# Expert 0's last row blocks between its second-layer products, and expert 1's weight splits spread over two experts

## The chip, the cores and the metric

The kernel runs on one core of a Trainium2 chip. The metric is the device time of one execution in microseconds (us); the lower, the better. The engines are named as the profile names them: PE (TensorE), DVE (VectorE), ACT (ScalarE), POOL (GpSimd) and SP (SyncE, which issues most transfers).

## What is computed

A recurrent attention over 4 batches, 8 heads and 768 steps gives an array of 3,072 rows by 320 columns, and a layer of 8 experts follows it. Each row goes to the one expert with the highest gate score, and the result is scaled by that score's probability:

```python
logits = x @ w_gate
expert_idx = np.argmax(logits, axis=1)
...
for e in range(E):
    mask = expert_idx == e
    xe = x[mask]
    h = np.maximum(xe @ w1[e], 0.0)      # 320 -> 1024
    ye = h @ w2[e]                       # 1024 -> 320
    out[mask] = gate_w[mask, None] * ye
```

## The kernel before

The attention takes the first 378 us of the profiled execution and is not touched. Near its end it has prepared the first 256 rows of expert 0 and split that expert's first-layer weights. The change lies in `moe`, in the first two of its eight experts.

**One expert.** Each expert has up to 448 rows (four row blocks, q = 0 to 3: three of 128 and one of 64); the five experts with most rows take this many and the others 384. Rows and weights are float32, and PE multiplies them in a faster format that drops low bits, so each operand is split into a rounded high part and the remainder, and three products replace one.

- `split(e)` returns seven pieces: three `s1(k)` for the first-layer weights and four `s2(k)` for the second. Each piece is one copy on ACT (L892 or L896, the high part) and one subtraction on DVE (L893 or L897, the low part). The raw weights come into `w1r` and `w2r` (`load_w1`, `load_w2`: L828, L833, L836). There is one buffer of each, so the transfer for the next expert waits until the last piece of this one has read it.
- `xprep(e, q)` turns one row block: three transposes on PE (L909) into one of two PSUM buffers `xt`, then in a chain ACT (L910, high part of the first 256 columns), DVE (L911, low part), ACT (L913, last 64 columns), DVE (L914).
- `l1(e, g, r)`, g = 0 to 3, is a quarter of the first layer, two blocks of 128 hidden units over the rows r: 16 products on PE (L927 to L931), then for each block a relu on ACT (L933) and the low part on DVE (L937).
- `l2(e, q)` is the second layer of one row block: 24 products (L949 to L951), and 16 for the block of 64 rows (L954 to L957). DVE scales the result (L964; L960 for the block of 64, after ACT's L959), and POOL writes the rows out by an indirect transfer (L965).
- `check(i)` reads an eighth of the raw decay array through the one buffer `WR` (L975, 480 KB) and takes its minimum and maximum on DVE (L976, L977). `within` is six short DVE operations (L877 to L882). Both feed a flag that is read only at the end.

**What sets the order.** In `moe`, the order of PE, ACT and DVE is the order of the program (`manual_schedule`), and each runs its list in that order. SP and POOL are not in that list: a planner places their instructions. The exception is the first `load_w1(1)`.

**The opening.** Expert 0's first 256 rows go through `l1(0, g, slice(0, 256))`, and behind each quarter one piece of that expert's second-layer weights is split. Then come `l2(0, 0)` and `l2(0, 1)`, the range check 0, `xprep` of row blocks 2 and 3, the first layer over rows 256 to 447, and then for each q one `xprep(1, q)`, two pieces of expert 1's split, and (q = 2, 3) the second layer of expert 0. From expert 1 on, the first layer covers all rows at once; two pieces of the next expert's split stand behind each quarter, and one `xprep` of the next expert stands before each `l2`.

Of the kernel before, what the change touches and what calls it, by code (L numbers as in the profile page):

```python
# [24 lines left out]
E = 8  # L25
# [760 lines left out]
def moe(tc, nc, d, ctx, X, out, okt, okv, oki, slots, first, cnts, consts, weights):  # L786
# [27 lines left out]
    def ps(tag, bufs):  # L814
        return PS.tile([128, 512], F32, name="m_" + tag, tag=tag, bufs=bufs)
# [3 lines left out]
    rows = lambda e: CAP if e < NBIG else SMALL  # L819

    def fetch(e):
        at[e] = nc.values_load(perm[0:1, e:e + 1], engines={mybir.EngineType.SP}, min_val=0, max_val=E - 1,
                               skip_runtime_bounds_check_because="perm is a permutation of the experts")

    def load_w1(e):
        w1 = d["w1"][which(e)]
        for k in range(2):
            x = DMA.dma_start(w1r[k], w1[:, k * 128:k * 128 + 128].rearrange("o p f->p (o f)"))  # L828
            if e == 1 and k == 0:
                tc.add_manual_dep(x.ins, gathered[-1].ins.name, mybir.DependencyInfo(  # L830
                    mybir.DependencyClass.Sync, mybir.DependencyReason.DATA))
        for h in (0, 64):
            DMA.dma_start(w1r[2][h:h + 64], w1[:, 256:320].rearrange("o p f->p (o f)"))  # L833

    def load_w2(e):
        DMA.dma_start(w2r, d["w2"][which(e)].rearrange("o (k p) m->p (o k) m", p=128))  # L836

    def load_w(e):
        load_w1(e)
        load_w2(e)  # L840

    def load_x(e):
        for q in range(0 if e else 2, (rows(e) + 127) // 128):
            ix = first[:, q - 2:q - 1] if e == 0 else idx[:, e, q:q + 1]
            x = G_.indirect_dma_start(out=XG[e % 2][:, q, :], out_offset=None, in_=X[0:NT + 1],
                                      in_offset=IndirectOffsetOnAxis(ap=ix.bitcast(U32), axis=0),
                                      bounds_check=NT, oob_is_err=False)
            if e == 0:
                gathered.append(x)
# [37 lines left out]
    def split(e):  # L887
        w1h, w1l = W1[e % 2]
        w2h, w2l = W2[e % 2]

        def s1(k):
            A.copy(w1h[k], w1r[k])  # L892
            V.tensor_tensor(w1l[k], w1r[k], f(w1h[k]), ALU.subtract)  # L893

        def s2(k):
            A.copy(w2h[:, k:k + 2], w2r[:, k:k + 2])  # L896
            V.tensor_tensor(w2l[:, k:k + 2], w2r[:, k:k + 2], f(w2h[:, k:k + 2]), ALU.subtract)  # L897

        return [lambda k=k: s1(k) for k in range(3)] + [lambda k=k: s2(k) for k in range(0, 8, 2)]

    def xprep(e, q):
        xg = XG[e % 2]
        xh, xl, x2 = XH[e % 2]
        n = 128 if q < 3 else 64
        cs = slice(q * 128, q * 128 + n)
        t = ps("xt", 2)[:, 0:384].rearrange("p (k i)->p k i", k=3)
        for k in range(3):
            kw = 128 if k < 2 else 64
            TE.transpose(t[:kw, k, 0:n], xg[0:n, q, k * 128:k * 128 + kw], ident[0:n, 0:n])  # L909
        A.copy(xh[:, :, cs], t[:, 0:2, 0:n])  # L910
        V.tensor_tensor(xl[:, :, cs], t[:, 0:2, 0:n], f(xh[:, :, cs]), ALU.subtract)  # L911
        yield
        A.copy(x2[0:64, 0, cs], t[0:64, 2, 0:n])  # L913
        V.tensor_tensor(x2[64:128, 0, cs], t[0:64, 2, 0:n], f(x2[0:64, 0, cs]), ALU.subtract)  # L914
        if q * 128 + n == rows(e):
            V.tensor_copy(tok[e % 2][:, 0 if e else 2:q + 1], xg[:, 0 if e else 2:q + 1, DM])
# [23 lines left out]
    def l2(e, q):  # L940
        w2h, w2l = W2[e % 2]
        n = 128 if q < 3 else 64
        qs = slice(q * 128, q * 128 + n)
        yp = ps("yp", 2)[:, 0:DM]
        sc = (xg0 if e == 0 and q < 2 else XG[e % 2])[:, q, DM + 1:DM + 2]
        yo = YO[q % 2]
        for ft in range(8):
            if n == 128:
                TE.matmul(yp, hh[:, ft, qs], w2h[:, ft], start=ft == 0, stop=False)  # L949
                TE.matmul(yp, hh[:, ft, qs], w2l[:, ft], start=False, stop=False)  # L950
                TE.matmul(yp, hl[:, ft, qs], w2h[:, ft], start=False, stop=ft == 7)  # L951
            else:
                if ft:
                    TE.matmul(yp[0:n], hh[:, ft, qs], w2l[:, ft], start=False, stop=False)  # L954
                TE.matmul(yp, hx[:, ft, 384:512], w2h[:, ft], start=ft == 0, stop=ft == 7)
                if not ft:
                    TE.matmul(yp[0:n], hh[:, ft, qs], w2l[:, ft], start=False, stop=False)  # L957
        if n < 128:
            A.activation(yt, yp[64:128], AF.Copy, scale=sc[64:128])  # L959
            V.scalar_tensor_tensor(yo[0:n], yp[0:n], sc[0:n], yt, ALU.mult, ALU.add)  # L960
        elif e == E - 1 and q == 2:
            A.activation(yo, yp, AF.Copy, scale=sc)
        else:
            V.tensor_scalar(yo, yp, sc, None, ALU.mult)  # L964
        x = G_.indirect_dma_start(  # L965
            out=out, out_offset=IndirectOffsetOnAxis(ap=tok[e % 2][0:n, q:q + 1].bitcast(U32), axis=0),
            in_=yo[0:n], in_offset=None, bounds_check=NT - 1, oob_is_err=False)
        for y in written:
            tc.declare_no_dep(x.ins, y.ins, reason="they write different rows")
        written.append(x)  # L970
# [3 lines left out]
    def check(i):  # L974
        DMA.dma_start(WR, d["w_raw"][:, i * n:(i + 1) * n])  # L975
        V.tensor_reduce(st[:, i:i + 1], WR, AX.X, ALU.min)  # L976
        V.tensor_reduce(st[:, E + i:E + 1 + i], WR, AX.X, ALU.max)  # L977

    def verdict(last):
        if not last:  # L980
            V.tensor_scalar(st[:, 0:E], st[:, 0:E], WLO, None, ALU.is_ge)
            V.tensor_scalar(st[:, E:2 * E], st[:, E:2 * E], WHI, None, ALU.is_le)
            V.tensor_reduce(okt[:, 1:2], st, AX.X, ALU.min)
            return
        p = ps("xt", 2)[0:1, 0:3]
        TE.matmul(p, okv[:, 0:1], okt, start=True, stop=True)
        V.tensor_reduce(okv[0:1, 1:2], p, AX.X, ALU.min)
        V.tensor_scalar(oki, okv[0:1, 1:2], 127.5, None, ALU.is_ge)

    with tc.manual_schedule(engines={mybir.EngineType.PE, mybir.EngineType.Activation, mybir.EngineType.DVE}):  # L990
        load_w2(0)
        DMA.dma_start(ident, d["cident"])
        load_x(0)
        order()
        for g in range(4):
            l1(0, g, slice(0, 256))
            split(0)[3 + g]()
        V.tensor_copy(tok[0][:, 0:2], xg0[:, :, DM])
        parts = [xprep(0, q) for q in (2, 3)]
        for q in range(2):  # L1000
            l2(0, q)
        check(0)
        for x in parts:
            next(x)
        for x in parts:
            next(x, None)
        for e in range(E):
            todo = split(e + 1) if 0 < e < E - 1 else []
            for g in range(4):
                l1(e, g, slice(0 if e else 256, rows(e)))  # L1010
                if e == E - 1 and g == 0:
                    check(e)
                for _ in range(2):
                    if todo:
                        todo.pop(0)()
            if e == 0:
                load_w2(1)
                todo = split(1) + [within]
            elif e + 2 < E:
                fetch(e + 2)  # L1020
                load_w(e + 2)
            for q in range((rows(e) + 127) // 128):
                if e + 1 < E and q * 128 < rows(e + 1):
                    list(xprep(e + 1, q))
                    if e == 0:
                        for _ in range(2):
                            if todo:
                                todo.pop(0)()
                elif e == E - 1 and q:
                    verdict(q == 2)  # L1030
                if e or q > 1:
                    l2(e, q)
                if q == 0 and 0 < e < E - 1:
                    check(e)
            if e == 0:
                fetch(2)
                load_w(2)
            if e + 2 < E:
                load_x(e + 2)

# [131 lines left out]
```

## Time and profile before

| | |
|---|---|
| device time, median of 3 runs | 609.2 us (607.48 to 609.25) |
| device time of the profiled execution | 605.91 us |
| its span (first to last instruction) | 604.1 us |
| PE busy in the span | 526.7 us, 87% |
| DVE, ACT, POOL busy | 423.0, 383.1, 262.3 us |
| granted PE clock, mean over the span | 0.947 |

The span is what the trace covers; 1.81 us of the profiled execution's time lie around it. In a line of a timeline, the time in square brackets is how long the engine stood idle before that line, and behind the arrow stands what it waited for. Products on PE overlap, so the distance from one start to the next, and not the duration shown, is what one costs when they follow closely.

### The profile page before, as it was taken

How to read it: one execution, taken by the hardware profiler on the slowest of the kernel's cores; microseconds unless marked ns; L12 is line 12 of the kernel's file. 1: busy time of each engine (PE TensorE's matmuls, PEld its weight loads, DVE VectorE, ACT ScalarE, POOL GpSimd, SP SyncE). 2: the span in 40 equal slices, each digit the busy share in tenths (PEclk: the TensorE clock that was granted, in tenths of full speed). 3: DMA queues.
4: the chain of work that ended last, by engine and by line, in shares of the span. 5: the costliest groups of instructions: out<-in, count | busy, mean ns of one | idle time of the engine just before them, and what ended most of it. 6: DMA issues, size and time to landing. Idle time of an engine off the chain costs nothing.

```text
span 604.1 us, 22198 instructions
## 1 busy us (share of the span) xinstructions
PE 526.7 (87%) x9302; PEld 476.2 (79%) x9311; DVE 423.0 (70%) x732; ACT 383.1 (63%) x931; POOL 262.3 (43%) x417
## 2 busy tenths in 40 slices
PE   1787888885998989799899988987999999999995
PEld 0546777775887888689788887986999999999994
DVE  8998986786698788757356465647848576676741
ACT  4666878897788889958778774325634435263420
POOL 5233578448949847964623023611141322314101
PEclk9997879998799999969879999889999999999998
DMA  7622454363445545443735345644756473645100
GB/s 212 204 78 82 145 151 151 116 190 93 154 126 158 164 125 152 137 134 92 187 90 155 86 130 193 182 164 118 248 166 205 128 223 115 194 127 185 55 9 33
DMA packets 37422, 85.50 MB, mean 142 GB/s; under 512 B 6173, under 2 KB 18206, under 8 KB 37316
## 3 DMA queue, kind: packets, MB, share of 16 engines
q1 hardware_dynamic: 34340, 74.93, 41.5%
q0 software_dynamic: 2704, 8.75, 4.5%
q8 instruction: 76, 1.25, 0.8%
q10 hardware_dynamic: 272, 0.33, 0.1%
q14 instruction: 30, 0.25, 0.1%
HBM read 76.07 MB, written 8.32 MB: 140 GB/s over the span
## 4 chain that ended last, share of the span: by engine, by line
PE 58%; DVE 17%; POOL 8%; issue 7%; DMA 5%; ACT 4%; SPq 1%; POOLq 0%; DVEq 0%; ACTq 0%
PE m_hp L928 4%; PE m_hp L929 4%; PE m_hp L927 4%; PE m_yp L949 4%; PE m_yp L951 4%; PE m_yp L950 4%; PE psY L518 4%; PE ps_g L495 3%; PE psS L427 3%; DVE G L296 2%; POOL tmp L364 2%; DVE FF L294 2%; PE psS L455 2%; PE m_hp L930 2%; PE m_hp L931 2%
## 5 line engine op out<-in xcount | busy, mean ns | idle before, releaser
L965 POOL DMA_INDIRECT out<-yo,tok x29 | 28.7, 991 | 152.9 <-DVE yo L964 106.9
L933 ACT ACTIVATE hx<-m_hp 128x448 fp32r<-128x448 f32 (+3 forms) x72 | 34.8, 485 | 48.5 <-PE m_hp L931 48.5
L949 PE MATMUL m_yp<-w2h,hx 128*128 128x320 f32 x192 | 60.8, 317 | 0.0
L951 PE MATMUL m_yp<-w2h,hx 128*128 128x320 f32 x192 | 59.1, 308 | 0.0
L950 PE MATMUL m_yp<-w2l,hx 128*128 128x320 f32 x192 | 59.1, 308 | 0.0
L937 DVE SCALAR_TENSOR_TENSOR hx<-m_hp,hx 128x384 fp32r<-128x384 f32 (+2 forms) x112 | 40.5, 402 | 22.8 <-ACT hx L933 22.3
L498 DVE TENSOR_TENSOR Y<-ps_g,mask 64x512 f32<-64x512 f32 x48 | 32.9, 685 | 21.7 <-PE ps_g L495 21.1
L325 ACT COPY M2c<-ps_g 32x256 f32<-32x256 f32 x96 | 34.9, 364 | 20.6 <-PE ps_g L317 19.0
L460 DVE TENSOR_TENSOR SVR<-psS,F 40x640 f32<-40x640 f32 x46 | 37.8, 822 | 11.5 <-PE psS L455 8.4
L418 ACT COPY KS<-ps_g 64x320 f32<-64x320 f32 x96 | 40.4, 421 | 8.3 <-PE ps_g L414 6.1
L303 POOL TENSOR_TENSOR lend<-lend,FF 128x1024 f32<-128x1024 f32 x12 | 28.5, 2372 | 38.4 <-DVE FF L294 32.9
L364 POOL TENSOR_TENSOR tmp<-Tt 128x28 f32<-128x28 f32 (+6 forms) x70 | 40.8, 583 | 4.9
L446 ACT COPY SVS<-psU 32x320 f32<-32x320 f32 x96 | 40.0, 417 | 4.5 <-PE psU L442 2.7
L471 ACT COPY KS<-ps_g 40x320 f32<-40x320 f32 x92 | 38.5, 419 | 2.8 <-PE ps_g L467 1.3
L518 PE MATMUL psY<-Y,KS 128*40 128x32 f32 x1504 | 34.2, 203 | 5.3 <-DVE Y L498 2.3
L296 DVE TENSOR_TENSOR_SCAN G<-Wt,RC 128x528 f32<-128x528 f32 x21 | 38.1, 1816 | 0.7
L518 PEld LDWEIGHTS psY<-Y,KS 128*40 128x40 f32 x1504 | 31.3, 122 | 8.4 <-issue 4.5
L455 PE MATMUL psS<-SVS,KS 128*40 128x40 f32 x1472 | 33.9, 208 | 3.0 <-ACT SVS L446 1.6
L950 PEld LDWEIGHTS m_yp<-w2l,hx 128*128 128x128 f32 x192 | 36.1, 188 | 0.0
L949 PEld LDWEIGHTS m_yp<-w2h,hx 128*128 128x128 f32 x192 | 36.0, 188 | 0.0
L951 PEld LDWEIGHTS m_yp<-w2h,hx 128*128 128x128 f32 x192 | 36.0, 187 | 0.0
L495 PE MATMUL ps_g<-RT,VU 128*64 128x64 f32 x768 | 31.2, 237 | 4.7 <-DMA Wt<-in_W 2.4
(248 smaller groups left out, 1532.9 us busy)
## 6 DMA issues: line engine op xcount, KB each, us to landing
w2r<-in_w SPq DMA_DIRECT2D x8, 1280.0 KB
lend<-in_w SPq DMA_DIRECT2D x16, 512.0 KB
VU<-in_VT SPq DMA_DIRECT2D x48, 160.0 KB
SVR<-in_VR SPq DMA_DIRECT2D x48, 104.0 KB
SVS<-in_VS SPq DMA_DIRECT2D x24, 208.0 KB
lend<-in_w SPq DMA_DIRECT2D x16, 256.0 KB
RT<-in_RT SPq DMA_DIRECT2D x48, 80.0 KB
Y<-in_RY SPq DMA_DIRECT2D x24, 160.0 KB
```

The source lines that it names most:

```text
L296: V.tensor_tensor_scan(back(at(G, s)), back(w), back(RC), 0.0, ALU.mult, ALU.max)
L364: V.tensor_tensor(t, bcast(0, j, 32, 0), bcast(j, j + 1, 0, 1), ALU.mult)
L418: A.copy(halves(ks[0:64, u * 8 + z:u * 8 + 8:2]), halves(ts[u][64 * z:64 * z + 64]))
L446: A.copy(halves(sv[32:64, 4 * v:4 * v + 4]), by_type(solved[32 * v:32 * v + 32]))
L455: TE.matmul(psS[TR[ty], h, j * 40:j * 40 + 40], ks[:, p, o:o + 40], sv[:, p, o:o + 40], start=True, stop=True, tile_position=(0, o))
L471: A.copy(ks[64:104, 8 * z:8 * z + 8, TO[ty]:TO[ty] + 40], ts[ty][64 * z:64 * z + 40])
L495: TE.matmul(a[z:z + 64, :, x], vu[:, p, :], rt[:, :, p, :], start=True, stop=True, tile_position=(0, z))
L518: TE.matmul(py[TR[ty], p], ks[:, p, o:o + 40], y2[:, ty, p, :], start=True, stop=True, tile_position=(0, o))
L937: V.scalar_tensor_tensor(o[:, ft, a - b:c - b], hp[:, a - r.start:c - r.start], 0.0, f(hh[:, ft, a:c]), ALU.max, ALU.subtract)
L949: TE.matmul(yp, hh[:, ft, qs], w2h[:, ft], start=ft == 0, stop=False)
L950: TE.matmul(yp, hh[:, ft, qs], w2l[:, ft], start=False, stop=False)
L951: TE.matmul(yp, hl[:, ft, qs], w2h[:, ft], start=False, stop=ft == 7)
```

## The change

- `l2(0, 0)` moves ahead of the preparation of expert 0's row blocks 2 and 3, and `l2(0, 1)` behind it.
- Range check 0 leaves the opening. It now stands behind `l2(1, 2)`, after check 1.
- The seven split pieces of expert 1 were all issued between the `xprep(1, q)`. Now the three of the first layer stand behind quarters 1 to 3 of expert 0's last first layer, two of the second layer between `xprep(1, 1)` and `l2(0, 2)`, and the last two behind quarter 0 of expert 1's first layer. The pieces of expert 2 follow one quarter later than before; the last three stand behind quarter 3.
- `xprep(1, 0)` and `xprep(1, 1)` come together before `l2(0, 2)`, and `xprep(1, 2)` and `xprep(1, 3)` together before `l2(0, 3)`.
- `load_w2(2)` is called in quarter 1 of expert 1 and no longer next to `load_w1(2)`, because `w2r` is read until then.
- `within` moves to expert 1, behind `xprep(2, 0)`.

```diff
         V.tensor_copy(tok[0][:, 0:2], xg0[:, :, DM])
+        l2(0, 0)
         parts = [xprep(0, q) for q in (2, 3)]
-        for q in range(2):
-            l2(0, q)
-        check(0)
         for x in parts:
             next(x)
         for x in parts:
             next(x, None)
+        l2(0, 1)
+        todo = []
         for e in range(E):
-            todo = split(e + 1) if 0 < e < E - 1 else []
+            todo = todo + split(e + 1) if e + 1 < E else []
+            if e == 1:
+                todo.append(within)
             for g in range(4):
                 l1(e, g, slice(0 if e else 256, rows(e)))
                 if e == E - 1 and g == 0:
                     check(e)
-                for _ in range(2):
+                if e == g == 1:
+                    assert len(todo) == 8
+                    load_w2(2)
+                for _ in range(2 + (e == 1 and g == 3) if e else int(g > 0)):
                     if todo:
                         todo.pop(0)()
             if e == 0:
                 load_w2(1)
-                todo = split(1) + [within]
             elif e + 2 < E:
                 fetch(e + 2)
                 load_w(e + 2)
             for q in range((rows(e) + 127) // 128):
-                if e + 1 < E and q * 128 < rows(e + 1):
+                if e == 0:
+                    if q > 1:
+                        for z in (2 * q - 4, 2 * q - 3):
+                            list(xprep(1, z))
+                        for _ in range(2 * (q == 2)):
+                            todo.pop(0)()
+                elif e + 1 < E and q * 128 < rows(e + 1):
                     list(xprep(e + 1, q))
-                    if e == 0:
-                        for _ in range(2):
-                            if todo:
-                                todo.pop(0)()
+                    if todo:
+                        todo.pop(0)()
                 elif e == E - 1 and q:
                     verdict(q == 2)
                 if e or q > 1:
                     l2(e, q)
                 if q == 0 and 0 < e < E - 1:
                     check(e)
+                elif q == 2 and e == 1:
+                    check(0)
             if e == 0:
                 fetch(2)
-                load_w(2)
+                load_w1(2)
```

## Rows read from the trace of the kernel before

**Rows 1.** Windows: length, busy us of PE, PEld, DVE, ACT, POOL, clock, DMA, GB/s.
```profile
396.10:400.60 4.50, 2.28 (x18) 2.11 (x19) 3.53 (x9) 0.97 (x5) 0.99 (x1) 1.00 0.72 244
400.60:404.00 3.40, 3.40 (x18) 3.40 (x18) 0.84 (x4) 0.73 (x3) 0.00 (x0) 0.50 0.10 40
...
416.30:419.60 3.30, 0.60 (x3) 0.25 (x2) 2.52 (x6) 1.75 (x5) 0.04 (x1) 1.00 0.67 160
419.60:432.50 12.90, 12.90 (x64) 11.84 (x65) 11.67 (x28) 9.68 (x16) 4.19 (x4) 1.00 0.78 256
432.50:447.10 14.60, 14.60 (x103) 14.21 (x102) 8.86 (x20) 3.42 (x10) 5.83 (x6) 1.00 0.59 190
```

**Rows 2.** Waits of PE from 420 us to the end: us, times, longest.
```profile
PE m_hp L928 <- DVE x L911: 1.0, 1, 1.0
```

**Rows 3.** Timeline of PE from the end of expert 0's first row blocks to expert 1.
```profile
395.23 0.81 PE L909 MATMUL m_xt<-mident,xg 128*128 128x128 f32 x6
...
398.68 0.36 PE L928 MATMUL m_hp<-x,lend 128*128 128x192 f32 x1 [1.93 <-DVE x L911]
...
407.42 0.82 PE L909 MATMUL m_xt<-mident,xg 128*128 128x128 f32 x6
409.49 0.52 PE L909 MATMUL m_xt<-mident,xg 128*128 128x128 f32 x3 [1.25 <-issue]
...
416.07 0.30 PE L955 MATMUL m_yp<-w2h,hx 128*128 128x320 f32 x1
418.07 0.47 PE L927 MATMUL m_hp<-x,w1h 128*128 128x448 f32 x1 [1.70 <-ACT x L910]
419.54 0.47 PE L928 MATMUL m_hp<-x,w1h 128*128 128x448 f32 x1 [1.00 <-DVE x L911]
```

**Rows 4.** Timeline of DVE, opening.
```profile
396.95 1.14 DVE L977 TENSOR_REDUCE rst<-wr 128x1 f32<-128x960 f32 x1
398.01 0.61 DVE L911 TENSOR_TENSOR x<-m_xt,x 128x256 fp32r<-128x256 f32 x2
...
408.35 0.42 DVE L911 TENSOR_TENSOR x<-m_xt,x 128x256 fp32r<-128x256 f32 x1
409.10 0.28 DVE L914 TENSOR_TENSOR x<-m_xt,x 64x128 fp32r<-64x128 f32 x1 [0.33 <-ACT x L913]
410.05 2.36 DVE L893 TENSOR_TENSOR w1l<-lend,w1h 128x1024 fp32r<-128x1024 f32 x2 [0.66 <-ACT w1h L892]
...
418.74 0.54 DVE L964 TENSOR_SCALAR yo<-m_yp,xg 128x320 f32<-128x320 f32 x1
419.20 0.28 DVE L911 TENSOR_TENSOR x<-m_xt,x 128x128 fp32r<-128x128 f32 x1
```

**Rows 5.** Groups by form, 378 to 450 us: count, busy us, mean ns, idle before.
```profile
L897 DVE TENSOR_TENSOR w2l<-w2r,w2h 128x640 fp32r<-128x640 f32 x12 | 9.7, 820 | 1.1 <-ACT w2h L896 1.1
...
L937 DVE SCALAR_TENSOR_TENSOR hx<-m_hp,hx 128x64 fp32r<-128x64 f32 x17 | 3.6, 213 | 0.0
...
L933 ACT ACTIVATE hx<-m_hp 128x192 fp32r<-128x192 f32 x8 | 2.6, 331 | 6.4 <-PE m_hp L931 6.4
L892 ACT CAST w1h<-lend 128x1024 fp32r<-128x1024 f32 x3 | 3.0, 1045 | 0.0
...
L937 DVE SCALAR_TENSOR_TENSOR hx<-m_hp,hx 128x128 fp32r<-128x128 f32 x8 | 2.3, 292 | 5.7 <-ACT hx L933 5.7
```

**Rows 6.** Timeline of SP's queue: transfers issued.
```profile
421.24 0.39 SPq L836 DMA_DIRECT2D w2r<-in_w  x1
...
439.23 0.34 SPq L975 DMA_DIRECT2D wr<-in_w_raw  x1
```

**Rows 7.** Timeline of ACT: the first piece of expert 2's second-layer split.
```profile
427.86 0.73 ACT L896 CAST w2h<-w2r 128x640 fp32r<-128x640 f32 x1 [0.16 <-DMA w2r<-in_w]
```

**Rows 8.** The indirect transfers of rows, from issue to landing.
```profile
DMA to landing us min/median/max: 2.9/3.8/7.2
```

**Rows 9.** Waits of SP's queue, 370 to 460 us: us, times, longest.
```profile
SPq L828 <- DVE w1l L893: 26.0, 3, 13.2
```

## The prediction

> **What bounds the kernel now.** Read the windows first: from 419.6 to 447.1 us PE is busy all of the time at the full clock [rows 1], and the list of PE's waits from 420 us to the end has a single entry, the tail of the last hole below [rows 2]. So behind 420 us the experts run at PE's pace, and a shift of the start of expert 2 shifts the end by as much, as long as nothing new makes PE wait. Before that, PE's timeline shows three holes and the windows one stretch at the low clock [rows 1, 3]. They are what the change can win:
>
> - Hole 1. The six transposes of expert 0's blocks 2 and 3 start at 395.23 and take 0.81, to 396.04; the second product of the first layer behind them starts at 398.68. One product costs 0.11 here (8.74 us from 398.68 to 407.42, less 1.7 us lost to the clock, over 63 products). The loss is 2.64 - 0.11 = 2.5 us. DVE's timeline shows why: the low parts (L911) start at 398.01, right behind the second of check 0's two reductions of 1.14 us each [rows 4].
> - The clock. After this hole the clock is 0.50, the lower of its two levels, for 3.4 us [rows 1]. Half of that, 1.7 us, is lost.
> - Hole 2. Two blocks of `xprep(1, q)` start at 407.42 and the third waits 1.25 us for a PSUM buffer [rows 3], which is free when DVE's L914 of the first has run, at 409.38 [rows 4].
> - Hole 3. The last second-layer product of expert 0 starts at 416.07, the second product of expert 1 at 419.54. Less one product of each kind (0.15 from 14.6 us over about 100 PE instructions, 0.20 from 12.9 us over 64, [rows 1]) this is 3.1 us. Its last releaser is L911 of block 3 at 419.20, behind splits and a scaling on DVE [rows 4].
>
> Together 2.5 + 1.7 + 1.25 + 3.1 = 8.55 us.
>
> **The change part by part.** PE's products and transposes stay the same in number, and so do the pieces, reductions and transfers; only their order differs. So I walk the three ordered queues through the new order, with the durations of the rows.
>
> *The opening.* `l2(0, 0)` ends at about 391.7 (half of the stretch before 395.23, each of its 24 products at 0.15). The transposes follow, and the chain of L910 to L914 runs while PE does the 3.5 us of `l2(0, 1)`. On DVE only one scaling of 0.54 stands ahead; the chain of a block is 1.03 us from L911 to the end of L914 (408.35 to 409.38, [rows 4]), so two fit. Cover gone, it would cost what hole 1 costs now. PE ends `l2(0, 1)` at 396.04 as before and goes straight on. Hole 1 goes, and with the idle time the stretch at the low clock: 2.5 + 1.7.
>
> *First-layer pieces in quarters 1 to 3.* 64 products at 0.112 are 7.2 us, 1.79 a quarter. ACT has two relus of 0.33 and a copy of 1.05, 1.71 in all; DVE has low parts of 2 x (0.29 + 0.21) and a subtraction of 1.18 (2.36 for two), less some 0.1 that each of these shares with the next one, about 1.9 [rows 4, 5]. Both are nearly full, neither is far behind: PE ends at 403.2, ACT copies the last piece until 404.7, DVE subtracts it by 405.95.
>
> *Expert 1's row blocks.* PE goes on with transposes, 24 products, transposes and 16 products. The work of this stretch, 407.42 to 416.22, is 8.8 less the wait of 1.25, so PE can be through at 403.2 + 7.55 = 410.75. The third transpose finds its buffer free, since `l2(0, 2)` now stands ahead: hole 2 goes, up to 0.2. DVE: from 405.95 two blocks of 1.03 (408.0), two second-layer pieces of 0.82 (409.7), the scaling (410.2), block 2 (411.25), L911 of block 3 at 0.28 (411.5). The second product of expert 1 wants that at 410.95. Hole 3 shrinks from 3.1 to 0.6. Bounds: 0 if DVE catches up anywhere, 3.1 if nothing is won. I take 0.6, from the walk.
>
> *Expert 1's first layer.* It starts 8.0 us earlier than now and takes 12.9 us of PE, to 424.4. The last two pieces of its own split follow quarter 0 (done on DVE by 417.6), and only then can the transfer of `w2r` for expert 2 start. Its row: issued at 421.24, waited for until 427.86, 6.62 us [rows 6, 7]. So it lands at 424.2. Its first reader on ACT stands behind quarter 2 and is due at 422.8: ACT waits 1.4 us there, and behind it in ACT's queue are the relus of quarter 3. PE needs these when `l2(1, 0)` comes to the seventh of its eight blocks, at 424.4 + 0.4 for the transposes + 18 x 0.147 = 427.4; they are done at 425.8. The cover is 1.6 us, and every us of lateness beyond it is one of PE's.
>
> *Expert 1's second layer.* This is where the displaced work lands. PE takes 14.6 us for it [rows 1], to 439.0. DVE has behind quarter 3 the rest of expert 2's pieces (to 428.95), `xprep(2, 0)` (429.9), `within` (six operations, at the 0.16 us that I estimate from the 0.21 of the smallest form in rows 5, 430.8), scaling (431.3), check 1 (433.45), block 1 and scaling (434.9), block 2 (435.85), the scaling of `l2(1, 2)` which PE ends at 436.35 (436.9), check 0 (439.05), L911 of block 3 (439.35). PE wants that at 439.2. DVE is exactly full, and check 0 has a condition of its own: its buffer is free only at 433.45, and the transfer then has 3.4 us. For its landing there are two rows: 2.9 us, the smallest of the indirect transfers of 162 KB (their median is 3.8) [rows 8], and 6.62 us for the 1,280 KB of `w2r`. The first costs PE 0.15, the second 3.4. By size, 480 KB lies at 3.8 + 2.8 x (480 - 162) / (1280 - 162) = 4.6 us, so I take 1.35. In the kernel before the same buffer is reloaded for a check a whole expert later [rows 6], so no row shows this wait.
>
> *Behind that* no expert changes, and `within` and the checks are read only at the end.
>
> **Sum.** 8.55 - 0.6 - 1.35 = 6.6 us. The profiled execution goes from 605.91 to 599.3. The median of the runs is 3.3 us above it; I take the same 6.6 off it: 602.6 us.
>
> **A rule against it.** The stretch at 0.50 follows 2.5 us of idle PE, while after 3.1 us in hole 3 the clock stays at 1.00 [rows 1]; so idle time does not by itself fix the loss. The Trainium skill ("TensorE: Matmul & The Clock Gate", section "Part 1: The HAM clock gate (the "warmup" mystery)") says that what decides on the clock runs free of the kernel and meets it at another point in each execution. By the rows the change wins 1.7 us here; by the page that part belongs to this one execution, and a sum without it would be 4.9 us, which is the first rival.
>
> **The rivals.**
>
> *The clock falls all the same.* The idle time left (0.6 before expert 1, 1.35 before expert 2) could bring another 3.4 us at half speed, or the runs before mostly lacked the fall. For it: rows 1 show both outcomes after holes of like length. Against it: what is left is shorter than either. It gives 602.6 + 1.7 = 604.3.
>
> *Check 0's transfer lands as late as that of `w2r`.* PE then waits 3.4 us before expert 2: 604.7, with a fall of the clock 606.4. For it: the transfer shares the DMA engines with the raw weights of expert 3, asked for only a few us earlier. Against it: it has 0.37 of the bytes.
>
> *Slower: `load_w2(2)` goes out behind the first-layer load of expert 3.* SP's order is the planner's. If it puts it there, SP stands as it does now at L828 until DVE has subtracted the last first-layer piece [rows 9], here at 424.2, and `w2r` lands near 432, 7.8 late. The relus behind its reader reach PE at 433.3 where 427.4 was wanted, DVE's chain shifts likewise, and with the wait for check 0's data expert 2's second product comes at 448.4, where it is now at 447.3: 1.1 slower, and 1.7 more as PE stands for 5.9 us: 612.0. It decides from a landing at about 431 on. Against it: in the program the call stands ahead of expert 3's.
>
> *No change.* The same transfer, held up by half as much beside others or in SP's queue, lands near 430 and takes back nearly all: 608 to 610.
>
> **How the numbers follow.** Chances: the forecast 0.60, the clock 0.15, the late check 0.12, no change 0.06, slower 0.07. 0.3% (1.8 us) is about what a measurement can tell from no change. The first three are faster by more: 0.87. The likeliest's own range is from 600.8 (holes all gone, 0.15 before expert 2) to 604. The whole range reaches from 600.0, as the runs before spread by 1.8 us, to 606.5, with the late check and the clock in it, and leaves out the last two cases.
>
> **What the trace will show.** Right: the second product of expert 0's last first layer starts near 396.2 with no wait, the clock stays at 1.00 from there, the third transpose of expert 1 waits less than 0.3, expert 1 starts near 411, expert 2 near 440.5, and the one new wait of PE stands there, released by L911 behind L977. Wrong would be: a wait of PE inside `l2(1, 0)` on ACT's relu (`w2r` late), a wait over 1 us before expert 1 (ACT and DVE too full in the quarters), or a low clock again near 400.

## The result

Over 22 runs each the changed kernel has a median of 605.04 us (595.95 to 610.53) and the kernel before 611.25 (602.25 to 617.6). The ratio is 0.9894, with a 95% interval of 0.9851 to 0.9937: 1.1% faster, 3.9 to 9.1 us by the interval, with 6.2 us between the medians. The ratios in this document leave out runs over 1.5% above the fastest of their kernel, while the medians count every run. The forecast was 6.6 us, and 602.6 us against a median of 609.2 that three runs had given; 605.04 lies in the range of 600.0 to 606.5.

The changed kernel was profiled twice, with spans of 608.7 and 603.1 us; the lines below are from the second, unless the first is named. The attention ends at another point in each execution, so distances within the experts are compared, not absolute times.

PE's timeline of the changed kernel, answering to [rows 3]:

```profile
400.31 0.26 PE L927 MATMUL m_hp<-x,lend 128*128 128x192 f32 x1
400.40 0.27 PE L928 MATMUL m_hp<-x,lend 128*128 128x192 f32 x1
...
407.43 0.82 PE L909 MATMUL m_xt<-mident,xg 128*128 128x128 f32 x6
...
412.28 0.36 PE L909 MATMUL m_xt<-mident,xg 64*128 64x64 f32 x3 [0.17 <-PE m_xt L909]
...
415.43 0.47 PE L927 MATMUL m_hp<-x,w1h 128*128 128x448 f32 x1 [0.25 <-ACT x L913]
415.91 0.47 PE L928 MATMUL m_hp<-x,w1h 128*128 128x448 f32 x1
...
443.32 0.37 PE L927 MATMUL m_hp<-x,lend 128*128 128x448 f32 x1
445.94 0.47 PE L928 MATMUL m_hp<-x,lend 128*128 128x448 f32 x1 [2.25 <-DVE x L911]
```

Hole 1 (2.5 us) is gone: the second product follows the first by 0.09. Of hole 2 (1.25) 0.17 is left, of hole 3 (3.1) some 0.5: 0.25 before the first product of expert 1, and 0.28 more than the usual 0.2 before the second. One new wait stands before the second product of expert 2. These are all of PE's waits from there to the end, as the list of PE's waits from 400 us says, answering to [rows 2]:

```profile
PE m_hp L928 <- DVE x L911: 2.3, 1, 2.3
PE m_hp L927 <- ACT x L913: 0.2, 1, 0.2
PE m_xt L909 <- PE m_xt L909: 0.2, 1, 0.2
```

The windows (columns as in [rows 1]) show the clock at full speed through the last first layer of expert 0, where it stood at half speed for 3.4 us, and the new wait in the last of them:

```profile
400.30:407.40 7.10, 7.10 (x66) 7.10 (x65) 4.28 (x15) 3.99 (x9) 0.99 (x1) 1.00 0.14 52
407.40:415.30 7.90, 7.61 (x54) 6.92 (x53) 6.50 (x15) 4.20 (x11) 0.43 (x1) 1.00 0.74 199
415.30:428.90 13.60, 13.45 (x65) 12.12 (x66) 10.37 (x22) 8.05 (x14) 3.57 (x4) 1.00 0.55 178
428.90:446.10 17.20, 14.95 (x103) 14.20 (x102) 13.07 (x28) 5.45 (x14) 6.15 (x6) 1.00 0.68 212
```

What follows the new wait differs between the two profiles. In the second the clock stays at 1.00. In the first, where the wait is 2.49 us, it falls behind the wait. PE's timeline in the first profile, and then a window behind the wait in the first and in the second:

```profile
449.97 0.47 PE L928 MATMUL m_hp<-x,lend 128*128 128x448 f32 x1 [2.49 <-DVE x L911]
```

```profile
449.90:453.50 3.60, 3.53 (x10) 3.16 (x11) 1.13 (x5) 1.28 (x3) 1.63 (x2) 0.56 0.67 200
```

```profile
445.90:460.50 14.60, 14.56 (x75) 13.50 (x76) 11.76 (x26) 10.39 (x18) 1.95 (x2) 1.00 0.57 169
```

From the second product of expert 2 to that of expert 3 the first profile takes 29.10 us (449.97 to 479.07) and the second 27.55: the fall costs 1.55 us.

**Two distances** serve as a measure from here on, read from PE's timeline in the same way everywhere. A runs from the second product of expert 0's last first layer to that of expert 1, and holds holes 2 and 3. B runs from there to the second product of expert 2, and holds the new wait, but not a fall of the clock behind that wait.

| kernel (profile) | A, us | B, us |
|---|---|---|
| before | 20.86 | 27.54 |
| before, again | 20.87 | 29.09 |
| changed, first profile | 15.53 | 30.25 |
| changed, second | 15.51 | 30.03 |
| before, check 0 at the end | 19.24 | 29.10 |
| opening part alone | 19.15 | 27.64 |
| splits part alone | 17.23 | 27.58 |
| changed, check 0 with its own buffer | 15.51 | 28.65 |
| changed, check 0 at the end (two profiles) | 15.51, 15.51 | 27.58, 27.54 |
| the same, expert 1's weights later (two) | 15.51, 15.50 | 27.58, 27.56 |
| before, expert 1's weights later | 20.87 | 29.06 |
| expert 2's second layer late | 15.51 | 31.69 |

The values repeat to 0.1 us, except where the clock falls or the new wait stands (30.03 and 30.25): A is 20.9 with a low clock behind hole 1 and 19.2 without, and B is 29.1 with one behind hole 3 and 27.6 without. 27.6 is the value with no hole, and 15.5 holds the 0.7 us that are left of holes 2 and 3.

### The profile page after: what moved, and what is told of

The parts are those of the page before. It is cut to its first block, busy times and chain, and to the rows that moved or that the text cites. A ratio compares the mean times of both kernels' runs of the same rounds, so it can differ in the third digit from the quotient of the medians.

```text
span 608.7 us, 22215 instructions
## 1 busy us (share of the span) xinstructions
PE 534.0 (88%) x9311; PEld 481.1 (79%) x9311; DVE 421.8 (69%) x732; ACT 383.3 (63%) x931; POOL 261.7 (43%) x417
## 3 DMA queue, kind: packets, MB, share of 16 engines
q8 instruction: 76, 1.25, 0.9%
## 4 chain that ended last, share of the span: by engine, by line
PE 53%; DVE 15%; POOL 10%; issue 7%; DMA 7%; ACT 6%; another core or an unknown queue 1%; SPq 0%; POOLq 0%; DVEq 0%; ACTq 0%
PE m_yp L950 4%; PE m_yp L949 4%; PE m_hp L928 4%; PE m_yp L951 4%; PE m_hp L927 4%; PE m_hp L929 4%; PE psY L518 3%; POOL tmp L364 3%; POOL Tt L366 3%; PE psS L427 3%; PE ps_g L495 2%; PE psS L455 2%; PE m_hp L931 2%; PE m_hp L930 2%; DVE SVR L460 2%
## 5 line engine op out<-in xcount | busy, mean ns | idle before, releaser
L949 PE MATMUL m_yp<-w2h,hx 128*128 128x320 f32 x192 | 62.2, 324 | 1.1 <-issue 1.1
L950 PE MATMUL m_yp<-w2l,hx 128*128 128x320 f32 x192 | 60.4, 315 | 0.9 <-DVE w2l L897 0.9
L951 PE MATMUL m_yp<-w2h,hx 128*128 128x320 f32 x192 | 60.1, 313 | 0.0
L518 PE MATMUL psY<-Y,KS 128*40 128x32 f32 x1504 | 36.3, 209 | 5.7 <-DVE Y L498 2.5
L518 PEld LDWEIGHTS psY<-Y,KS 128*40 128x40 f32 x1504 | 33.4, 128 | 8.8 <-issue 4.7
L949 PEld LDWEIGHTS m_yp<-w2h,hx 128*128 128x128 f32 x192 | 36.9, 192 | 1.7 <-issue 1.5
L455 PEld LDWEIGHTS psS<-SVS,KS 128*40 128x40 f32 x1472 | 32.0, 125 | 7.2 <-issue 4.1
L364 POOL TENSOR_TENSOR tmp<-Tt 128x28 f32<-128x28 f32 (+6 forms) x70 | 35.5, 507 | 4.9
L951 PEld LDWEIGHTS m_yp<-w2h,hx 128*128 128x128 f32 x192 | 36.9, 192 | 0.0
```

Of the source, the lines that this page charges most:

```text
L364: V.tensor_tensor(t, bcast(0, j, 32, 0), bcast(j, j + 1, 0, 1), ALU.mult)
L455: TE.matmul(psS[TR[ty], h, j * 40:j * 40 + 40], ks[:, p, o:o + 40], sv[:, p, o:o + 40], start=True, stop=True, tile_position=(0, o))
L518: TE.matmul(py[TR[ty], p], ks[:, p, o:o + 40], y2[:, ty, p, :], start=True, stop=True, tile_position=(0, o))
```

## The experiments

### The changed kernel again

> The changed kernel once more. In the first profile of it ACT and DVE stood still for 4 us before the third quarter's second block of expert 0 (389 to 393 us), and the clock fell behind that. Theory 1 (an accident of that execution): both are gone here; from the first product of expert 0 to the second product of expert 2 it takes 69.3 (before) - 8.55 + 0.3 + 2.7 = 63.8 us, give or take 1, with no low clock behind the first quarters. Theory 2 (the new order brings the stop about, since the transfers run against it): it is there again, and this stretch takes 69 us again. In both the wait for check 0's data before expert 2 is about 2.5 us.

Ratio to before 0.9907 (0.9861 to 0.9952), 605.87 us. From the first product of expert 0 to the second product of expert 2 it takes 66.4 us (379.51 to 445.94), where theory 1 said 63.8 and theory 2 said 69. The stop is there again, a little elsewhere, so it was not an accident of the one execution; but the same stop also showed in the next experiment, with the old order. So neither theory holds as it was put. ACT's timeline, first profile and then second:

```profile
392.33 0.38 ACT L933 ACTIVATE hx<-m_hp 128x256 fp32r<-128x256 f32 x1 [3.99 <-remote]
```

```profile
391.02 0.39 ACT L933 ACTIVATE hx<-m_hp 128x256 fp32r<-128x256 f32 x1 [2.09 <-remote]
393.21 0.39 ACT L933 ACTIVATE hx<-m_hp 128x256 fp32r<-128x256 f32 x1 [1.80 <-remote]
```

"Remote" means that the profile knows no releaser. The products were there (in the first profile the block's last one started at 388.35), and ACT did not start. In the second profile PE waits 2.49 and 0.45 us for the second-layer split behind it, which is what the 66.4 us have over theory 1 to within 0.3, and no low clock follows. This lies ahead of A and B.

### Check 0 alone moved away

```diff
         for q in range(2):
             l2(0, q)
-        check(0)
...
                 if e == E - 1 and g == 0:
                     check(e)
+                if e == E - 1 and g == 2:
+                    check(0)
```

> The kernel before, with range check 0 alone moved, to quarter 2 of the last expert. Theory 1 (the two reductions were hole 1): DVE is free when the transposes end, but the chain of the two row blocks still stands between transposes and first layer; hole 1 shrinks from 2.5 to about 1.1 us, holes 2 (1.25) and 3 (3.1) stay; with the clock's 1.7 us, if it does not fall after the shorter hole, 3.1 us are won, 1.4 us if it falls. Theory 2 (the order of the row blocks was hole 1, not the reductions): it stays at 2 us or more, and nothing is won.

Ratio 0.9945 (0.9897 to 0.9993). PE's timeline of this kernel:

```profile
396.35 0.81 PE L909 MATMUL m_xt<-mident,xg 128*128 128x128 f32 x6
397.51 0.36 PE L927 MATMUL m_hp<-x,lend 128*128 128x192 f32 x1 [0.35 <-ACT x L910]
397.95 0.35 PE L928 MATMUL m_hp<-x,lend 128*128 128x192 f32 x1
```

The second product starts 0.79 us after the transposes, less 0.11 for one product: 0.7 us of hole 1 are left of 2.5. So the two reductions were 1.8 us of it, and only the last 0.7 need the products around the preparation. The clock does not fall behind this short hole, and A drops by 1.62 to 19.24, the price of the fall. But it falls behind hole 3 instead, where it had not fallen before: of the 14.4 us of expert 1's first layer the mean clock is 0.88.

```profile
417.30:431.70 14.40, 14.40 (x64) 13.11 (x65) 11.76 (x28) 9.54 (x16) 4.14 (x4) 0.88 0.74 235
```

### Check 0 moved away in the changed kernel

The same edit on the changed kernel, whose call of check 0 in expert 1 goes.

> The changed kernel, with range check 0 moved from expert 1 to quarter 2 of the last expert, where DVE is half idle. Theory 1 (the check with its late transfer is all of the new wait): the wait before expert 2 (2.5 us idle) is gone, and the kernel is 2.5 to 2.7 us faster than the changed one. Theory 2 (DVE is over-full behind expert 1 from the displaced splits, with or without the check): 1 us or more of the wait stays.

Ratio 0.9856 (0.9769 to 0.9943), and in a second set of runs 0.9913 (0.9877 to 0.9949). B is 27.58 and 27.54, the value of the kernel before: the new wait is gone entirely. PE's waits from the last first layer of expert 0 to the end, in the second profile:

```profile
PE m_hp L927 <- ACT x L910: 0.3, 1, 0.3
PE m_xt L909 <- PE m_xt L909: 0.2, 1, 0.2
```

So theory 1 holds for the wait: the displaced splits alone do not overfill DVE. That the kernel is 2.5 to 2.7 us faster than the changed one is not shown by the times, since the interval (0.9769 to 0.9943) holds the changed kernel's ratio of 0.9907 in the same set of runs.

### A buffer of its own for check 0

```diff
+    WR0 = P.tile([128, n], F32, name="wr0")
...
     def check(i):
-        DMA.dma_start(WR, d["w_raw"][:, i * n:(i + 1) * n])
+        t = WR if i else WR0
+        DMA.dma_start(t, d["w_raw"][:, i * n:(i + 1) * n])
...
```

> The changed kernel, check 0 in the same place but with a buffer of its own, so that its transfer is asked for early. Theory 1 (the late transfer is the larger half): DVE's 1.75 us wait for the data goes, the two reductions stay, and the wait of PE before expert 2 shrinks from 2.5 to between 0.2 and 1.0 us. Theory 2 (DVE's time is what counts): it stays above 1.5 us.

Ratio 0.9884 (0.9802 to 0.9967). B is 28.65: of the 2.5 to 2.7 us (30.03 and 30.25 against 27.54) 1.1 are left. So 1.4 to 1.6 us are the late transfer, and 1.1 us the reductions on a DVE that has no room for them. DVE's timeline of the changed kernel (second profile), and then of this one, where the extra declaration shifts the line numbers by one or two:

```profile
436.70 1.15 DVE L976 TENSOR_REDUCE rst<-wr 128x1 f32<-128x960 f32 x1
437.76 1.14 DVE L977 TENSOR_REDUCE rst<-wr 128x1 f32<-128x960 f32 x1
...
441.40 0.55 DVE L964 TENSOR_SCALAR yo<-m_yp,xg 128x320 f32<-128x320 f32 x1
443.47 1.15 DVE L976 TENSOR_REDUCE rst<-wr 128x1 f32<-128x960 f32 x1 [1.52 <-DMA wr<-in_w_raw]
444.54 1.14 DVE L977 TENSOR_REDUCE rst<-wr 128x1 f32<-128x960 f32 x1
445.60 0.28 DVE L911 TENSOR_TENSOR x<-m_xt,x 128x128 fp32r<-128x128 f32 x1
```

```profile
443.95 0.55 DVE L965 TENSOR_SCALAR yo<-m_yp,xg 128x320 f32<-128x320 f32 x1
444.42 1.14 DVE L978 TENSOR_REDUCE rst<-wr 128x1 f32<-128x960 f32 x1
445.48 1.14 DVE L979 TENSOR_REDUCE rst<-wr 128x1 f32<-128x960 f32 x1
446.54 0.28 DVE L912 TENSOR_TENSOR x<-m_xt,x 128x128 fp32r<-128x128 f32 x1
```

In the first, check 0 waits 1.52 us for its data with the last low part (L911) behind it in the queue; in the second the reductions follow the scaling at once, and L911 is still late for PE. The 1.1 us that are left are a little over the 1.0 that theory 1 allowed.

### Each half of the change alone

The first half: `l2(0, 0)` and `l2(0, 1)` around the preparation and check 0 in expert 1, with the splits of expert 1 as before.

```diff
+        l2(0, 0)
         parts = [xprep(0, q) for q in (2, 3)]
-        for q in range(2):
-            l2(0, q)
-        check(0)
...
+        l2(0, 1)
...
+                elif q == 2 and e == 1:
+                    check(0)
```

> The kernel before with the first half of the change alone: second-layer products around the preparation of blocks 2 and 3, check 0 in expert 1; expert 1's splits stay where they were. Theory 1 (the parts add up, and the new wait needs the displaced splits): hole 1 is gone, from the second product of expert 0's last first layer to that of expert 1 it takes 19.2 us as with the check moved alone (holes 2 and 3 stay), and before expert 2 PE waits under 0.5 us, since DVE comes to check 0 later than its data (freed by check 1 at once, landing 4.8 us later). Theory 2 (the wait is check 0's own): PE waits 2 us or more before expert 2.

Ratio 0.9963 (0.9918 to 1.0008). Hole 1 and the low clock behind it are gone, A is 19.15 and B 27.64; PE has no wait before expert 2. DVE comes to check 0 with nothing owed, and its data are there:

```profile
443.36 0.55 DVE L964 TENSOR_SCALAR yo<-m_yp,xg 128x320 f32<-128x320 f32 x1 [2.08 <-PE m_yp L951]
443.82 1.14 DVE L976 TENSOR_REDUCE rst<-wr 128x1 f32<-128x960 f32 x1
```

So the new wait needs both halves: here DVE waits for PE ahead of check 0 (2.08 us), in the whole change it runs behind it.

The second half: the changed kernel with check 0 and the two `l2` of the opening put back as they were.

> The kernel before with the second half of the change alone: the splits and row blocks of expert 1 in their new order; check 0 and the second-layer products of expert 0 in the opening as they were. Theory 1: hole 1 stays at 2.5 us, holes 2 and 3 shrink to 0.5 in all (15.5 us for that stretch, 17.1 if the low clock falls in it), no wait over 0.3 us before expert 2; 3.7 us are won in all. Theory 2 (DVE, still late from check 0, hands the delay on to the pieces in the quarters): hole 3 stays above 1.5 us.

Ratio 0.9931 (0.9896 to 0.9967). A is 17.23, which is 15.5 and the fall of the clock behind hole 1, and B 27.58. PE's waits from the transposes of expert 0 to the end:

```profile
PE m_hp L928 <- DVE x L911: 1.9, 1, 1.9
PE m_hp L927 <- ACT x L910: 0.6, 2, 0.4
PE m_xt L909 <- PE m_xt L909: 0.2, 1, 0.2
```

The first line is hole 1, unchanged. Holes 2 and 3 shrink without help from the other half.

### The kernel before, again

> The kernel before once more, for the place where the low clock falls and for the stop of ACT that four of the other profiles show near expert 0's third and fourth quarter (relu L933, some 4 us). Theory 1 (clock and stop belong to the execution, not to the order): the holes are those of before (2.5, 1.25, 3.1 us), but the 3.4 us at half clock need not stand behind hole 1, and the stop may appear. Theory 2 (both follow from the order): the low clock stands again behind hole 1, and there is no stop.

One execution of 607.04 us. The three holes are the same, and the clock falls twice, behind hole 1 (A is 20.87) and behind hole 3:

```profile
398.20:407.00 8.80, 8.76 (x64) 8.76 (x65) 3.46 (x17) 2.55 (x9) 0.00 (x0) 0.81 0.19 59
...
419.10:423.40 4.30, 4.29 (x13) 3.82 (x14) 3.17 (x12) 1.89 (x4) 3.20 (x3) 0.60 0.40 97
```

Theory 1 holds for hole 3 only. ACT does not stop. Behind hole 1 at its full size the clock fell in all four profiles that have it (before twice, the splits alone, and expert 1's weights later); behind hole 3 at its full size in three of five.

### Expert 2's second-layer weights held back

On the kernel with check 0 at the end and expert 1's weights later (next section). The transfer waits for the second first-layer piece of expert 2:

```diff
                 if e == g == 1:
                     assert len(todo) == 8
-                    load_w2(2)
                 for _ in range(2 + (e == 1 and g == 3) if e else int(g > 0)):
                     if todo:
-                        todo.pop(0)()
+                        late = todo.pop(0)()
+                if e == g == 1:
+                    load_w2(2, late)
...
```

> The kernel with check 0 at the end and late expert 1 weights, but expert 2's second-layer transfer held back until the second first-layer piece of expert 2 is subtracted, some 4.2 us later than now. Theory 1 (relus stand behind the reader in ACT's queue, and 1.6 us are covered): ACT waits for the data 6 us instead of 2, and PE has a new wait of 2.4 to 3 us inside the second layer of expert 1, at its seventh block, so that the stretch between the second products of experts 1 and 2 grows from 27.6 to 30 to 31 us. Theory 2 (PE has work enough): no wait there, and 27.6 us as before.

Ratio 0.9922 (0.9894 to 0.9951). B is 31.69, 4.1 us more than 27.58. ACT's timeline, PE's waits and the windows:

```profile
426.67 0.72 ACT L896 CAST w2h<-w2r 128x640 fp32r<-128x640 f32 x1 [5.15 <-DMA w2r<-in_w]
427.30 0.97 ACT L933 ACTIVATE hx<-m_hp 128x448 fp32r<-128x448 f32 x2
```

```profile
PE m_yp L949 <- ACT hx L933: 1.7, 1, 1.7
PE m_yp L951 <- DVE hx L937: 0.3, 1, 0.3
```

```profile
424.00:428.00 4.00, 2.28 (x16) 2.02 (x15) 0.57 (x1) 1.33 (x3) 0.00 (x0) 1.00 1.06 413
428.00:434.00 6.00, 5.68 (x27) 5.33 (x28) 5.51 (x17) 2.94 (x7) 0.00 (x0) 0.72 0.57 156
```

The wait is where theory 1 put it, inside the second layer on a relu that stands behind the waiting copy. The waits themselves are 2.0 us; a fall of the clock to a mean of 0.72 over 6 us takes 1.7 more, which makes up most of the rest. The wait is smaller than the 2.4 to 3 us expected, since ACT waited 5.15 us and not 6, and the stretch is longer than the 30 to 31 us expected, since the fall of the clock was not in the expectation. With the transfer where the change puts it, ACT waits 2 us as well (1.98 in the second profile) and PE none. So the cover that the prediction counted on is real and of that size: ACT can wait 5.15 - 2.0 = 3.1 us before PE feels it, where the walk had 1.4 + 1.6 = 3.0.

### Expert 1's weights later

On the changed kernel with check 0 at the end: expert 1's first-layer transfer is asked for only when expert 0's four quarters are through.

```diff
-        with tc.manual_schedule(engines={mybir.EngineType.SP}):
-            fetch(1)
-            load_w1(1)
...
-        V.tensor_copy(tok[0][:, 0:2], xg0[:, :, DM])
+        gathered.append(V.tensor_copy(tok[0][:, 0:2], xg0[:, :, DM]))
+        with tc.manual_schedule(engines={mybir.EngineType.SP}):
+            fetch(1)
+            load_w1(1)
```

> The changed kernel with check 0 at the end, and expert 1's first-layer transfer asked for only when expert 0's four quarters are split, so that the DMA engines are not full during these quarters. Theory 1 (the stop of ACT comes from something that shares the DMA engines with this 1.5 MB transfer): no stop in the quarters; the kernel is 1 to 4 us faster than with check 0 at the end alone in those executions that had one. Theory 2 (the stop is independent of these transfers): it shows here as well, and the time is that of check 0 at the end. In both the transfer lands some 2 us before its first reader, so that no new wait stands in quarters 1 to 3 of the last first layer.

Ratio 0.9864 (0.9808 to 0.9919), 598.98 us beside 602.08 for the kernel with check 0 at the end, in two sets of runs that are not of the same time. No stop shows, and the span is 593.4 us. So both were run again, side by side:

> The changed kernel with check 0 at the end and expert 1's first-layer transfer behind expert 0's quarters, once more beside the next. Theory 1 (this transfer, early, brings the stop of ACT about): again no stop of ACT or DVE in the quarters in the profile, and a median below the next kernel's by 1 us or more. Theory 2 (chance): stop or no stop as in the next, and medians within 1 us of each other.

> The changed kernel with check 0 at the end, once more: the stretch between the second products of experts 1 and 2 is 27.6 us again. Theory 1: a stop of ACT or DVE of 1.5 us or more near expert 0's last quarters or the scaling behind them. Theory 2: none.

Ratios 0.9902 (0.9867 to 0.9938) and 0.9913 (0.9877 to 0.9949), medians 598.17 and 598.20 us: no difference that these runs can show. Neither profile has a stop in the quarters. And on the kernel before:

> The kernel before with only expert 1's first-layer transfer moved behind expert 0's quarters. Theory 1: the three holes as before (2.5, 1.25, 3.1 us), no stop in the quarters, and since two of the three other profiles with the old splits' order show a stop or a shorter delay there, 1 to 3 us faster than the kernel before. Theory 2: no difference to the kernel before.

Ratio 0.9974 (0.9944 to 1.0004): no difference that this can show, though the interval leaves room for the 1 to 3 us of theory 1. No stop in the profile, and the holes as before. Taken together, ACT stops in expert 0's quarters or right behind them in six of ten profiles with the early transfer and in none of four with the late one, while the times side by side do not tell them apart. What causes the stop stays open.

## Why the prediction was right

**Hole 1 and the clock (2.5 + 1.7).** Right. The second product follows at once, and the clock is at 1.00 from there through the last first layer of expert 0, in both profiles. In the first there is a low clock near 400 us all the same, which the prediction named as a sign of being wrong (0.59 from 395 to 399 us); it follows ACT's stop and ends ahead of that product at 404.19. The parts were not told apart in the prediction: with the check away alone, 0.7 of the 2.5 us stay.

**Holes 2 and 3 (1.25 + 2.5 won).** Right in sum and in kind: without falls of the clock A goes from 19.24 to 15.51, 3.73 us against 3.75. The third transpose found its buffer free, and DVE was late by about 0.5 us where the walk said 0.6.

**The cover of the second-layer transfer.** Right: issued 6.3 us after the second product of expert 1 (422.25 less 415.91; in the walk 417.6 less 411.55, 6.05), waited for 1.98 us by ACT (walk 1.4), not felt by PE. Held back further, it is felt.

```profile
422.25 0.39 SPq L836 DMA_DIRECT2D w2r<-in_w  x1
425.36 1.47 SPq L828 DMA_DIRECT2D lend<-in_w  x2
...
438.93 7.12 SPq L975 DMA_DIRECT2D wr<-in_w_raw  x2
```

```profile
429.32 0.73 ACT L896 CAST w2h<-w2r 128x640 fp32r<-128x640 f32 x1 [1.98 <-DMA w2r<-in_w]
```

**The new wait (1.35).** The mechanism, the place and the landing were right, the size was not: 2.5 to 2.7 us. Check 0's transfer, issued at 438.93, had landed when its reader started at 443.47: 4.54 us (4.78 in the first profile), against 4.6 taken by size. The mis-sized term is DVE's own list, "exactly full" with 0.15 us over; it measured 1.1. The same lateness shows where check 1 frees the buffer: 22.99 us behind the second product of expert 1 in both profiles, where the walk had 21.9 (433.45 less 411.55). These 1.1 us and the 1.35 of the forecast make 2.45. Some 0.75 of them came with the second-layer data of expert 2: 7.07 us from issue to reader (422.25 to 429.32), where 6.62 was taken from [rows 6, 7], after an issue that was 0.3 us late. DVE passes that on to every piece behind it. The rest lies in DVE's pieces and is not told apart. With its own buffer for check 0 the kernel loses 1.1 us there, so the transfer's share came out at 1.4 to 1.6.

**What the sum left out.** Behind hole 3 the clock falls as well, in three of five executions, at 1.5 us each; the profile of before was one of the other two. That is about 0.9 us on average that the change wins besides. Against it stands the fall behind the new wait, 1.55 us in one of two executions, about 0.8 on average. With both the measured parts give 2.5 + 1.6 + 3.7 + 0.9 - 2.6 - 0.8 = 5.3 us. The interval of the ratio, 3.9 to 9.1 us, does not tell this from the 6.2 between the medians or the 6.6 forecast. So it is in part luck that the forecast's number was met so closely: the wait cost 1.2 more than was taken, and two falls of the clock that were not in the sum nearly cancel.

**The rivals.** That the clock falls all the same came true in one of the two profiles of the changed kernel, behind the new wait, at 1.55 us where 1.7 was taken; the times do not decide how often. That the 1.7 us behind hole 1 belong to one execution did not: the clock fell there four times of four. The Trainium skill ("TensorE: Matmul & The Clock Gate", section "Part 1: The HAM clock gate (the "warmup" mystery)") says that what decides on the clock runs free of the kernel, so that the same program meets it at another point in each execution. Hole 3, with three falls in five, agrees with that, and hole 1 shows no such difference. The late check did not land late. The second-layer transfer went out ahead of expert 3's (SP's lines above), so the slower rival had no start, though holding the same transfer back by 4.2 us showed that its price is real. That price was worked out from 447.3 us for expert 2's second product; the trace of before has 447.08, so the walk gives 1.3 us and not 1.1.

## What to carry to other kernels

Work that is moved off one stall lands in some other engine's list, and there it counts with everything else that the change moves to the same place: each half of this change alone costs nothing behind expert 1, and together they overfill DVE by 1.1 us, and waiting for check 0's transfer costs another 1.4 to 1.6. Work that only has to be done some time belongs where its engine is half idle: in the last expert check 0 costs PE nothing, and the kernel with it there took 0.986 and 0.991 of the time of before. The changed kernel took 0.989 and 0.991, so what this last step gains shows in B and not in the times. When one profile is the base of a sum, a loss that depends on the clock may be missing from it.

## What was not expected of the hardware

In seven of fourteen profiles, with the old order and the new, ACT stood still for 1.7 to 4 us, in one piece or two, before a relu whose input was ready for most of that time, and the profile names no releaser; six of these lie near expert 0's last quarters, one (2.60 us) in expert 2, where PE did not feel it. Near the quarters PE's waits behind it come to 1.8 to 3.3 us, and it can bring a fall of the clock behind it (0.59 from 395 to 399 us in the first profile of the changed kernel).
